# Layer-norm sums of 14 of 16 tiles made by ScalarE instead of VectorE, with a new order of operations, in an H3 and product-key-expert kernel

## The chip, the cores and the metric

One core of a Trainium2 chip runs the whole program. A core has five engines with a queue each, worked off in order: TensorE (PE in the profile; its weight loads are PEld), VectorE (DVE), ScalarE (ACT), GpSimd (POOL) and SyncE (SP). They run side by side and wait for one another by semaphores. Sixteen DMA engines move data between HBM and the core's memory SBUF; PE writes its products to PSUM. The metric is device microseconds (us) of one execution, lower is better.

## The reference: what is computed

The input `x` has 2048 tokens of 448 values. It is normalised over the 448 values, goes into two parts, and the output is the sum of `x` and both.

```python
xn = _layernorm(x)                         # (x - mean) / sqrt(var + 1e-5)
return x + _A_ref(xn, ...) + _B_ref(xn, ...)

# A: k gets a causal convolution of 4 taps, times v, then a causal convolution of
#    length 2048 in each channel by FFT, plus kv * ssm_D, times the gate xn
# B: 16 heads; s1, s2 = scores of xn's two query halves against 64 keys each
#    the best 2 of s1 and of s2 give 4 sums, the best 2 of these are the experts
g = _softmax(top_s)
act = _gelu(jnp.einsum("nd,nhkd->nhk", xf, u[top_e]))
out = jnp.einsum("nhk,nhk,nhkd->nd", g, act, v[top_e])
```

So every token reads 32 rows of `u` and 32 of `v` out of 4096.

## The kernel before

The tokens are 16 tiles (`T`) of 128. `acc` holds `x` and later the sum, `xn` the normalised input, both for all tiles. The program is straight code without loops on the chip; its order is made when it is built.

**Stages.** First the weights: the query projection is folded with the keys (L303 to L335) into `wh`, `wl` and `wr`, high and low halves of a 448 by 2048 matrix. Then the scores: for each tile `s_turn` transposes `xn` on PE (L347 into `px`), ACT splits it into `xh` and `xl` (L376 to L384), and `s_mm` makes four chunks of 512 scores (11 matmuls each, L363 to L367). `s_top` searches them on DVE: 8 times MAX8 (L407) and 8 times the index search (L405) a chunk. `s_pairs` picks the two experts of a head (L426 to L454), ACT makes the gates (`th`, `eg`, L434 to L437), PE places them (`pe`, L486), and ACT writes the rows' numbers `idx` and the gates `gt` (L469, L470). From then on POOL can gather a tile's rows.

Third come the experts, in 128 batches (8 a tile, named `b`). A batch is four gathers on POOL (L508) of 128 rows of `u` and `v` side by side, 0.46 MB each, into one of four buffers `uv`. DVE multiplies by the tokens' values (L540 for up to four gathers at once; L547 does one gather with its sum), ACT makes the sums (L559) and the gelu `ge` (L563), DVE the weight `w` (L574), ACT or DVE spreads it (`cc`, L589 or L579), PE adds up the rows of `v` (`pv`, L599 and L602), and with that the buffer is free. After a tile's last batch `vs`, `pf` and the sum into `acc` follow (L612, L621, L623).

Fourth, the convolution in two groups of 56 blocks of channels: SP loads `hkv` into `x1` (`c_load`, L639, seven loads of 0.8 MB, the first group's once the last tile's experts are placed), then taps, the transforms on PE and products of spectra on DVE (L738 to L744), the way back, and the gate into `acc`. The experts go on beside it.

**What sets the order.** Each stage is a stream of `Op`s with an engine, a cost in us, the keys that it waits for and a priority. `Planner.run` takes, engine by engine, the operation that can start first by these costs; among those that start within a little, the one with the smaller number in `PRIO`. The convolution's and the scores' numbers also change as the plan goes on: the scores are urgent while the gathers left to give out are fewer than `LEAD`, and `LATE` is added to the time at which a gather is taken to have landed before DVE's product is planned. The engines then do exactly that order; where data is late, all that stands behind it on the engine waits.

**What the change touches.** `norm(t0, t1)` normalises the tiles from `t0` to `t1`. It runs three times: tiles 0 and 1 ahead of all, tiles 2 to 5, and tiles 6 to 15. For each tile DVE makes mean and variance (L256 and L257); then, for the group at once, 3 + 16 + 1 small operations make `rstd` by Newton steps and `nmr` = -mean * rstd (L262 to L273, tiles `n`); then ACT writes `xn` tile by tile (L276).

```python
def stats(t=t):
    st = rp.tile([P, 6], F32, tag="st", name="st")
    nc.vector.bn_stats(st, acc[:, t, :])
    nc.vector.bn_aggr(mv[:, t, :], st)
yield Op("DVE", 0.78, stats, [("x", t0)])
```

Of the kernel before, what the change touches and what calls it, by code (L numbers as in the profile page):

```python
# [15 lines left out]
AF = mybir.ActivationFunctionType  # L16
ALU = mybir.AluOpType

P = 128
S, D, H, E = 2048, 448, 16, 64  # L20
# [6 lines left out]
VERBOSE = False  # L27
BEHIND = 0.2
PAD = 1.0
LEAD = 16  # L30
SPAN, AHEAD, WORK = 25.0, -0.010, 548.0


# [42 lines left out]

PRIO = {"c_back": 0.5, "c_delta": -0.1, "c_fin": 0.4, "c_fm": -0.4, "c_gate": -0.1, "c_hh": 0.5, "c_in": 0.5, "c_inv": 0.2, "c_mul": -0.2, "c_prod": -0.1, "c_spec": 0.3, "c_turn": 0.2, "c_zt": -0.5, "e_fold": -0.3, "e_gather": -0.5, "e_out": 0.5, "e_scale": -0.4, "e_spread": -0.5, "e_values": -0.5, "s_gate": 0.2, "s_put": -0.1, "s_top": 0.3, "s_turn": 0.1}


class Ring:
# [109 lines left out]
def parallel_kernel(ctx, tc, x, wq, kk, uv, hkv, const, fq, out):  # L192
    nc = tc.nc
# [14 lines left out]
    acc = ap.tile([P, NT, D], F32, name="acc")  # L208
    xn = ap.tile([P, NT, D], F32, name="xn")
# [5 lines left out]
    mv = ap.tile([P, NT, 2], F32, name="mv")  # L215
    rstd = ap.tile([P, NT], F32, name="rstd")
    nmr = ap.tile([P, NT], F32, name="nmr")
# [32 lines left out]
    def norm(t0, t1):  # L250
        sl, n = slice(t0, t1), t1 - t0
        va, y0, y1 = (ap.tile([P, n], F32, name=f"n{i}_{t0}") for i in range(3))
        for t in range(t0, t1):
            def stats(t=t):
                st = rp.tile([P, 6], F32, tag="st", name="st")
                nc.vector.bn_stats(st, acc[:, t, :])  # L256
                nc.vector.bn_aggr(mv[:, t, :], st)  # L257
            yield Op("DVE", 0.78, stats, [("x", t0)])


        def guess():
            nc.vector.tensor_scalar(va, mv[:, sl, 1], 1e-5, None, op0=ALU.add)  # L262
            nc.vector.tensor_scalar(y1.bitcast(I32), va.bitcast(I32), 1, None, op0=ALU.logical_shift_right)
            nc.vector.tensor_scalar(y0.bitcast(I32), y1.bitcast(I32), -1.0, float(0x5F3759DF), op0=ALU.mult, op1=ALU.add)
        yield Op("DVE", 0.5, guess)
        for i in range(4):
            def step(i=i):
                nc.vector.tensor_mul(y1, y0, y0)
                nc.vector.tensor_mul(y1, y1, va)
                nc.vector.tensor_scalar(y1, y1, -0.5, 1.5, op0=ALU.mult, op1=ALU.add)  # L270
                nc.vector.tensor_mul(y0 if i < 3 else rstd[:, sl], y1, y0)
            yield Op("DVE", 0.65, step)
        yield Op("DVE", 0.17, lambda: nc.vector.scalar_tensor_tensor(nmr[:, sl], mv[:, sl, 0], -1.0, rstd[:, sl], op0=ALU.mult, op1=ALU.mult),  # L273
                 key=("rstd", t0))
        for t in range(t0, t1):
            yield Op("ACT", 0.72, lambda t=t: nc.scalar.activation(xn[:, t, :], acc[:, t, :], AF.Identity, bias=nmr[:, t:t + 1], scale=rstd[:, t:t + 1]),  # L276
                     [("rstd", t0)], key=("xn", t))
# [253 lines left out]
    def e_dots():  # L531
        for b, (T, j, hf) in enumerate(order):
# [3 lines left out]
            if na:  # L536
                def go(b=b, T=T, j=j, na=na, begin=begin):
                    begin()
                    u = live["uv", b][:, :na, :D]
                    nc.vector.tensor_mul(u, live["xr", T, j][:, None, :D].broadcast_to([P, na, D]), u)  # L540
                yield Op("DVE", 0.1 + 0.46 * na, go, [(("land", b, na - 1), LATE), ("xr", T, j - j % 2)], key=("mul", b), rings=[(r_act, ("ge", b))])
            for c in range(na, 4):
                def go(b=b, T=T, j=j, c=c, na=na, begin=begin):
                    if c == 0:
# [3 lines left out]
                                                   accum_out=live["act", b][:, c:c + 1])  # L548
                yield Op("DVE", 0.63, go, [(("land", b, c), LATE), ("xr", T, j - j % 2)], key=("dot", b) if c == 3 else None,
                         rings=[(r_act, ("ge", b))] if c == 0 else [])  # L550
# [74 lines left out]
    def e_store(g):  # L625
        for T in range(NT):
            ch = slice(HALF * g, HALF * g + HALF)
            yield Op("SP", 0.06, lambda T=T: nc.sync.dma_start(out[T, :, ch], acc[:, T, ch]), [("sum", T), ("gt", g, GC // 8 - 1)], moved=1.15e5)
# [80 lines left out]
    def c_fm(g):  # L709
        for q in qs:  # L710
            def go(q=q):
                live["fm", g, q] = cp.tile([P, 2, P], F32, tag="fm", name="fm", bufs=FM)
                nc.sync.dma_start(live["fm", g, q].rearrange("p i n -> p (i n)"), fq[q])
            yield Op("SP", 0.06, go, [("cm", g, 4, 1)] if q == 0 else [], key=("fm", g, q), rings=[(r_fm, ("psu", g, q))], moved=1.35e5)

    def c_spec(g):

        for q in qs:
            def go(q=q):
                ps = live["psf", g, q] = ps_sc.tile([P, 512], F32, tag="sc", name="psf")  # L720
                nc.tensor.matmul(ps[:, :2 * HALF], live["fm", g, q][:, 0], x1[:, :, :, q, :].rearrange("p c t k -> p t c k"), start=True, stop=True)  # L721
            yield Op("PE", 0.85, go, [("fm", g, q)] + ([("x1", g, BC_LAST, t, 6) for t in range(2)] if q == 0 else []), key=("psf", g, q),
                     rings=[(r_sc, ("y", g, q))], lag=0.2)

    def c_hh(g):
        for q in qs:
            def go(q=q):
                hh = live["hh", g, q] = cp.tile([P, 2, HALF], F32, tag="hh", name="hh", bufs=HH)
                nc.scalar.activation(hh[:, 0], live["psf", g, q][:, :HALF], AF.Copy)
            yield Op("ACT", 0.28, go, [("psf", g, q)], key=("hh", g, q), rings=[(r_hh, ("psu", g, q))])  # L730
# [74 lines left out]

    LATE = 1.0
    r_ws, r_xh, r_eg, r_act, r_ge, r_w, r_cc, r_vs = Ring(2), Ring(2), Ring(2), Ring(3), Ring(3), Ring(3), Ring(2), Ring(1)
    live["by_act"], live["by_scale"] = 4, True  # L810
    nc.scalar.dma_start(kks, kk)
# [13 lines left out]
    plan.show("weights")  # L825
    experts = [plan.add(PRIO.get(s.__name__, 0.0), s()) for s in (e_gather, e_values, e_weigh, e_scale, e_spread, e_dots, e_gelu, e_out, e_fold)]
    stores = [plan.add(1, e_store(g)) for g in range(2)]
# [6 lines left out]
    def need(s):  # L834
        first = (0.2 if s in (s_mm, s_top) else 0.3 if s in (s_turn, s_split) else 0.4) - PRIO.get(s.__name__, 0.0)
        return lambda: (-1 if 32 * live["ready"] - plan.busy["POOL"] / 1.25 < LEAD else 2) - first
    plan.run([plan.add(need(s), s(pairs if s in (s_top, s_gate, s_place) else rest)) for s in scores])
# [11 lines left out]
    def turn():  # L849
        e = (plan.busy["POOL"] - begun) / (640.0 - begun)  # L850
        return -1 if plan.spent.get("conv", 0.0) / WORK < e + AHEAD else 1
    conv = []
    for g in range(2):
        for i, s in enumerate((c_load(g), c_delta(g), c_in(g, 0), c_store(g, 0), c_tap(g), c_prod(g), c_in(g, 1), c_store(g, 1),
                  c_fm(g), c_spec(g), c_hh(g), c_mul(g), c_inv(g), c_turn(g), c_back(g), c_zt(g), c_fin(g), c_gate(g))):
            conv.append(plan.add(lambda p=PRIO.get(s.__name__, 0.0): turn() + p, s, "conv"))
    plan.run(conv)
# [43 lines left out]
```

## Time and profile before

| | us |
|---|---|
| runs: median of 3 (lowest to highest) | 831.16 (830.13 to 832.6) |
| the profiled execution, its own time | 827.13 |
| its span, first to last instruction | 825.4 |
| scores of the first two tiles and norm of the rest | 57 to 82 |
| scores of tiles 2 to 15, experts beside them | 82 to 358 |
| convolution, group 0 then group 1, experts beside it | 358 to 825 |

The profile is of one execution. For each engine it gives busy time and instructions; a row of a group of instructions has line, engine, operation, output and inputs, count, then busy us and mean ns, then the idle time of the engine just before them and what ended it. A row of the timeline has start, duration, engine, line, operation, and in brackets the idle time before it with its releaser. Some views cut the span into stretches. In such rows `sc` are the scores, `mx` and `mi` maxima and indices, `n` the small tiles of the norm.

All 512 gathers together took this on POOL, with the idle time between them and what ended the most of it:

```profile
L508 POOL DMA_INDIRECT uv<-in_uv_dram,idx x512 | 491.5, 960 | 313.5 <-issue 95.6 <-ACT gt L470 67.0 <-PE pv L602 37.7
```

### The profile page before, as it was taken

What the parts mean: (1) busy time and instruction counts of PE and PEld (TensorE: products, weight loads), DVE (VectorE), ACT (ScalarE), POOL (GpSimd) and SP (SyncE); (2) the same over time, 40 slices, a digit from 0 to 9 for tenths busy, and PEclk for the clock granted to TensorE, in tenths of its full rate; (3) what the DMA queues carried; (4) which work ended last, traced back from release to release, by engine and by line L of the source; (5) the groups of instructions that cost most, each with busy time, mean ns of one, the idle gap of its engine ahead of it and who ended that gap; (6) DMA issues with size and microseconds to landing.
All of it is one profiled execution on the core that took longest, in us unless ns stands there. A gap on an engine that the chain in (4) does not pass through costs nothing.

```text
span 825.4 us, 16762 instructions
## 1 busy us (share of the span) xinstructions
PE 663.5 (80%) x5052; PEld 386.1 (47%) x5052; DVE 704.4 (85%) x2633; ACT 541.1 (66%) x1862; POOL 492.2 (60%) x518
## 2 busy tenths in 40 slices
PE   6994999899799999755876778886567878787884
PEld 2463565565456665413543343444244533333561
DVE  4379999999999999955898999984799779999774
ACT  4431897677777767665785676765378656766852
POOL 0004666576667666662777766666365776776670
PEclk9997799999999999976989999899698999999998
DMA  9955898899989998999999999999899999999995
GB/s 333 381 211 175 293 329 306 305 334 329 320 309 351 331 323 300 336 340 365 387 351 323 396 373 383 366 350 387 286 396 350 313 402 399 383 395 396 330 377 187
DMA packets 80554, 278.53 MB, mean 337 GB/s; under 512 B 10320, under 2 KB 47568, under 8 KB 80464
## 3 DMA queue, kind: packets, MB, share of 16 engines
q0 software_dynamic: 40960, 234.91, 77.2%
q1 hardware_dynamic: 39360, 42.41, 15.3%
q8 instruction: 41, 0.67, 0.3%
q14 instruction: 49, 0.40, 0.1%
q10 hardware_dynamic: 144, 0.13, 0.1%
HBM read 273.75 MB, written 3.67 MB: 336 GB/s over the span
## 4 chain that ended last, share of the span: by engine, by line
DVE 62%; PE 15%; DMA 14%; ACT 4%; issue 4%; DVEq 0%; SPq 0%; POOL 0%; POOLq 0%; ACTq 0%
DVE uv L540 21%; DVE mi L405 11%; DVE mx L407 7%; DMA uv<-in_uv_dram,idx 7%; DMA x<-in_hkv_dram 6%; PE pw L303 3%; ACT uv L559 3%; DVE hh L738 3%; DVE hh L739 3%; DVE hh L743 2%; PE pv L602 2%; PE ps L693 2%; DVE tap L660 2%; DVE tap L658 2%; DVE uv L547 2%
## 5 line engine op out<-in xcount | busy, mean ns | idle before, releaser
L508 POOL DMA_INDIRECT uv<-in_uv_dram,idx x512 | 491.5, 960 | 313.5 <-issue 95.6
L559 ACT ACTIVATE uv<-uv 128x448 f32<-128x448 f32 x455 | 256.5, 565 | 118.5 <-DVE uv L540 118.2
L540 DVE TENSOR_TENSOR uv<-xr,uv 128x1792 f32<-128x1792 f32 (+2 forms) x128 | 232.0, 1812 | 27.1 <-DMA uv<-in_uv_dram,idx 21.2
L602 PE MATMUL pv<-uv,cc 128*32 128x448 f32 x1024 | 140.6, 592 | 0.0
L405 DVE FIND_INDEX8 mi<-mx,sc 128x8 uint32<-128x64 f32 x512 | 105.4, 240 | 0.0
L753 PE MATMUL psu<-hh,fm 128*128 128x224 f32 x264 | 70.9, 396 | 21.2 <-DVE hh L744 18.1
L559 ACT ACTIVATION_READ_ACCUMULATOR uv<-uv 128x1 f32 x455 | 85.1, 187 | 0.0
L599 PE MATMUL pv<-uv,cc 128*1 128x4 bf16 x128 | 21.5, 168 | 79.0 <-DVE cc L579 63.0
L363 PE MATMUL sc<-wh,xh 128*128 128x512 f32 x192 | 82.1, 428 | 1.6 <-DVE mi L405 1.6
L753 PEld LDWEIGHTS psu<-hh,fm 128*128 128x128 f32 x264 | 48.8, 204 | 66.2 <-ACT uv L559 31.7
L407 DVE MAX8 mx<-sc 128x8 f32<-128x64 f32 x512 | 74.5, 230 | 3.1 <-PE sc L367 2.9
L365 PE MATMUL sc<-wh,xl 128*128 128x512 f32 x192 | 76.2, 397 | 0.0
L364 PE MATMUL sc<-wl,xh 128*128 128x512 f32 x192 | 76.2, 397 | 0.0
L693 PE MATMUL ps<-cst,x 128*64 128x132 f32 x896 | 64.4, 303 | 10.2 <-DVE x L675 6.3
L693 PEld LDWEIGHTS ps<-cst,x 128*64 128x64 f32 x896 | 56.4, 151 | 32.4 <-DVE x L675 8.2
L599 PEld LDWEIGHTS <-cc 128*1 128x1 bf16 x128 | 10.2, 80 | 129.0 <-DVE cc L579 92.0
L721 PE MATMUL psf<-x,fm 128*128 128x448 f32 x132 | 62.0, 563 | 0.4 <-DVE hh L744 0.2
L589 ACT ACTIVATE cc<-rep,w 128x32 f32<-128x32 f32 x196 | 46.4, 307 | 12.7 <-DVE w L574 12.6
L363 PEld LDWEIGHTS sc<-wh,xh 128*128 128x128 f32 x192 | 36.9, 192 | 34.1 <-issue 18.0
L405 DVE MATCH_VALUE_LOAD mi<-mx,sc 128x8 f32 x512 | 45.9, 90 | 0.0
L521 PE MATMUL xr<-xn,rep 32*128 32x448 f32 x128 | 34.5, 617 | 13.4 <-DVE uv L540 11.9
L761 ACT ACTIVATE x<-psu 128x224 f32<-128x224 f32 (+1 forms) x66 | 23.4, 354 | 27.9 <-PE psu L753 27.6
(98 smaller groups left out, 1028.3 us busy)
## 6 DMA issues: line engine op xcount, KB each, us to landing
wq<-in_wq_dram SPq DMA_DIRECT2D x16, 896.0 KB, 13.4
x<-in_hkv_dram SPq DMA_DIRECT2D x14, 780.0 KB, 14.8
fm<-in_fq_dram SPq DMA_DIRECT2D x66, 128.0 KB, 6.6
uv<-in_uv_dram,idx POOLq DMA_INDIRECT x512
out_dram<-acc SPq DMA_DIRECT2D x32, 112.0 KB, 1.8
acc<-in_x_dram SPq DMA_DIRECT2D x1, 2240.0 KB
acc<-in_x_dram SPq DMA_DIRECT2D x1, 896.0 KB
cst<-in_const_dram SPq DMA_DIRECT2D x1, 540.0 KB
```

Source lines behind the costliest of these rows:

```text
L363: nc.tensor.matmul(sc, xh[:, c, :], wh[:, c, ns], start=(c == 0), stop=False)
L364: nc.tensor.matmul(sc, xh[:, c, :], wl[:, c, ns], start=False, stop=False)
L365: nc.tensor.matmul(sc, xl[:, c, :], wh[:, c, ns], start=False, stop=False)
L405: nc.vector.max_index(mi[:, T % 2, 8 * n + j, :], m, sc[:, 64 * j:64 * j + 64])
L407: nc.vector.max(m, sc[:, 64 * j:64 * j + 64])
L508: made = nc.gpsimd.indirect_dma_start(live["uv", b][:, c, :], None, uv, bass.IndirectOffsetOnAxis(ap=idx[:, T, g:g + 1], axis=0)).ins
L540: nc.vector.tensor_mul(u, live["xr", T, j][:, None, :D].broadcast_to([P, na, D]), u)
L559: nc.scalar.activation(u, u, AF.Copy, accum_out=live["act", b][:, c:c + 1])
L602: nc.tensor.matmul(pv[32 * c:32 * c + 32, :D], cc[:, c, :], buf[:, c, D:], start=(hf == 0), stop=(hf == 1), tile_position=(0, 32 * c))
L693: nc.tensor.matmul(ps[64 * i:64 * i + 64, w * j:w * j + w], src, f1[:, i, :], start=True, stop=True, tile_position=(0, 64 * i))
L721: nc.tensor.matmul(ps[:, :2 * HALF], live["fm", g, q][:, 0], x1[:, :, :, q, :].rearrange("p c t k -> p t c k"), start=True, stop=True)
L753: nc.tensor.matmul(ps[:, :HALF], fm[:, 1], hh[:, i], start=(i == 0), stop=(i == 1))
```

## The change

For the two later groups of tiles `norm` no longer uses DVE's statistics. ACT reads a tile twice: a copy scaled by -1/448 whose accumulator gives minus the mean, and a square of the tile with that as its bias, whose accumulator gives the sum of squared differences. Both write their main output into `xn`, which the last step overwrites. The division by 448 goes into the first small operation on DVE, and the sign into the last; tiles 0 and 1 stay as they are. Two numbers of the planner and the table of priorities change too. The lines behind the new code are 12 further down.

```diff
-LEAD = 16
+LEAD = 12
...
-PRIO = {"c_back": 0.5, "c_delta": -0.1, "c_fin": 0.4, "c_fm": -0.4, "c_gate": -0.1, "c_hh": 0.5, "c_in": 0.5, "c_inv": 0.2, "c_mul": -0.2, "c_prod": -0.1, "c_spec": 0.3, "c_turn": 0.2, "c_zt": -0.5, "e_fold": -0.3, "e_gather": -0.5, "e_out": 0.5, "e_scale": -0.4, "e_spread": -0.5, "e_values": -0.5, "s_gate": 0.2, "s_put": -0.1, "s_top": 0.3, "s_turn": 0.1}
+PRIO = {"c_back": 0.5, "c_delta": -0.1, "c_fin": -0.1, "c_fm": -0.4, "c_gate": -0.1, "c_hh": 0.4, "c_in": 0.5, "c_inv": 0.2, "c_load": -0.4, "c_mul": -0.2, "c_prod": 0.1, "c_spec": 0.3, "c_store": 0.2, "c_tap": 0.5, "c_turn": 0.4, "c_zt": 0.3, "e_dots": 0.2, "e_fold": -0.3, "e_gather": -0.2, "e_gelu": -0.2, "e_out": -0.1, "e_scale": -0.3, "e_spots": -0.2, "e_spread": -0.5, "e_values": -0.5, "s_gate": 0.1, "s_put": -0.5, "s_split": 0.1, "s_top": 0.3, "s_turn": 0.1}
...
         for t in range(t0, t1):
+
+            def mean(t=t):
+                nc.scalar.activation(xn[:, t, :], acc[:, t, :], AF.Copy, scale=-1.0 / D, accum_out=mv[:, t, 0:1])
+            def squares(t=t):
+                nc.scalar.activation(xn[:, t, :], acc[:, t, :], AF.Square, bias=mv[:, t, 0:1], accum_out=mv[:, t, 1:2])
...
-            yield Op("DVE", 0.78, stats, [("x", t0)])
+            if t0 < 2:
+                yield Op("DVE", 0.78, stats, [("x", t0)])
+            else:
+                yield Op("ACT", 0.76, mean, [("x", t0)])
+                yield Op("ACT", 0.76, squares, key=("mv", t))
...
-            nc.vector.tensor_scalar(va, mv[:, sl, 1], 1e-5, None, op0=ALU.add)
+            if t0 < 2:
+                nc.vector.tensor_scalar(va, mv[:, sl, 1], 1e-5, None, op0=ALU.add)
+            else:
+                nc.vector.tensor_scalar(va, mv[:, sl, 1], 1.0 / D, 1e-5, op0=ALU.mult, op1=ALU.add)
...
-        yield Op("DVE", 0.5, guess)
+        yield Op("DVE", 0.5, guess, [("mv", t1 - 1)] if t0 >= 2 else [])
...
-        yield Op("DVE", 0.17, lambda: nc.vector.scalar_tensor_tensor(nmr[:, sl], mv[:, sl, 0], -1.0, rstd[:, sl], op0=ALU.mult, op1=ALU.mult),
+        yield Op("DVE", 0.17, lambda: nc.vector.scalar_tensor_tensor(nmr[:, sl], mv[:, sl, 0], -1.0 if t0 < 2 else 1.0, rstd[:, sl], op0=ALU.mult, op1=ALU.mult),
...
-    LATE = 1.0
+    LATE = 0.5
```

The order of the instructions is shown at three places. The first is ACT's queue from the split of tile 1 (`xh`, `xl_98`) to the first rows' numbers `idx`, before:

```order
L378 ACTIVATE xh<-px 64x128
L383 ACTIVATE xl_98<-px 128x384
L384 ACTIVATE xl_98<-px 64x128
L434 ACTIVATE th<-dd 128x16
L436 ACTIVATE eg<-th,half 128x16
L437 ACTIVATE eg<-th,half 128x16
L469 ACTIVATE idx<-pe 128x32
L470 ACTIVATE gt<-pe 128x32
```

and now:

```order
L390 ACTIVATE xh<-px 64x128
L256 ACTIVATE xn,mv<-acc 128x448
L258 ACTIVATE xn,mv<-acc,mv 128x448
...
L446 ACTIVATE th<-dd 128x16
L448 ACTIVATE eg<-th,half 128x16
L449 ACTIVATE eg<-th,half 128x16
...
L481 ACTIVATE idx<-pe 128x32
L482 ACTIVATE gt<-pe 128x32
```

Six tiles' means and squares (12 activations, with `xl_98` among them) now stand ahead of `th`, five activations between `eg` and `idx`, and the other 11 behind `gt`, around tile 1's `th` and `idx`.

The second is DVE's queue at the first products of the experts (`uv_751` is the second batch's, `uv_813` the third's; `w` are the weights), before:

```order
L574 TENSOR_TENSOR w_875<-ge_866,gt_90 128x4
L256 BN_STATS st_877<-acc_81 128x6
L257 BN_AGGR mv_86<-st_877 128x2
L256 BN_STATS st_894<-acc_81 128x6
L257 BN_AGGR mv_86<-st_894 128x2
L256 BN_STATS st_902<-acc_81 128x6
L257 BN_AGGR mv_86<-st_902 128x2
L256 BN_STATS st_906<-acc_81 128x6
L257 BN_AGGR mv_86<-st_906 128x2
L540 TENSOR_TENSOR uv_813<-xr_541,uv_813 128x4x448
L574 TENSOR_TENSOR w_937<-ge_919,gt_90 128x4
L262 TENSOR_SCALAR n0_6_538<-mv_86 128x10
```

and now, where `uv_759`, `uv_827` and `uv_866` are the second to fourth batch:

```order
L285 SCALAR_TENSOR_TENSOR nmr_88<-mv_86,rstd_87 128x10
L552 TENSOR_TENSOR uv_759<-xr_541,uv_759 128x4x448
L586 TENSOR_TENSOR w_883<-ge_869,gt_90 128x4
L552 TENSOR_TENSOR uv_827<-xr_541,uv_827 128x4x448
L586 TENSOR_TENSOR w_919<-ge_909,gt_90 128x4
L552 TENSOR_TENSOR uv_866<-xr_541,uv_866 128x4x448
L419 MAX mx_957<-sc_921 128x8 x4
L586 TENSOR_TENSOR w_966<-ge_952,gt_90 128x4
L419 MAX mx_957<-sc_921 128x8 x4
```

The statistics are gone between the products, and the small operations for tiles 6 to 15 are all done ahead of the second product instead of around the fourth. The weight of the third batch (`w_966`) now splits the first search of tile 2, so that search waits for ACT's gelu.

The third is DVE's queue in the scores of tile 3 (chunks `sc_1115`, `sc_1144`, `sc_1204`, `sc_1232`), before:

```order
L407 MAX mx_998<-sc_1115 128x8 x8
L540 TENSOR_TENSOR uv_1073<-xr_1010,uv_1073 128x4x448
L574 TENSOR_TENSOR w_1222<-ge_1202,gt_90 128x4
...
L540 TENSOR_TENSOR uv_1132<-xr_1010,uv_1132 128x4x448
...
L574 TENSOR_TENSOR w_1296<-ge_1276,gt_90 128x4
...
L540 TENSOR_TENSOR uv_1219<-xr_1315,uv_1219 128x4x448
L574 TENSOR_TENSOR w_1373<-ge_1338,gt_90 128x4
L405 MAX_INDEX mi_999<-mx_998,sc_1232 128x8 x8
```

and now (chunks `sc_1150`, `sc_1206`, `sc_1275`, `sc_1298`):

```order
L552 TENSOR_TENSOR uv_1032<-xr_970,uv_1032 128x4x448
L419 MAX mx_957<-sc_1150 128x8 x8
...
L552 TENSOR_TENSOR uv_1092<-xr_970,uv_1092 128x4x448
L586 TENSOR_TENSOR w_1234<-ge_1225,gt_90 128x4
...
L552 TENSOR_TENSOR uv_1164<-xr_1239,uv_1164 128x4x448
L586 TENSOR_TENSOR w_1289<-ge_1273,gt_90 128x4
...
L552 TENSOR_TENSOR uv_1221<-xr_1239,uv_1221 128x4x448
L586 TENSOR_TENSOR w_1337<-ge_1325,gt_90 128x4
...
L417 MAX_INDEX mi_958<-mx_957,sc_1298 128x8 x8
```

Four batches' products stand in tile 3's scores instead of three. The two orders are the same in this from here to the end of the scores: nine weights before tile 3's last search now, eight before; 48 before tile 15's last search now, 47 before. At the first product of the second group's spectra 99 batches are weighed instead of 100, at its first gate 120 in both.

## The prediction

> **What bounds the kernel now.** I read the page's busy shares and its chain first, then stretches of the span, and then single rows.
>
> ```profile
> PE 663.5 (80%) x5052; PEld 386.1 (47%) x5052; DVE 704.4 (85%) x2633; ACT 541.1 (66%) x1862; POOL 492.2 (60%) x518
> DVE 62%; PE 15%; DMA 14%; ACT 4%; issue 4%; DVEq 0%; SPq 0%; POOL 0%; POOLq 0%; ACTq 0%
> ```
>
> VectorE is busiest and carries most of the chain. The average hides stages, so the next view cuts the span: columns are the stretch, its length, busy time of PE, weight loads, DVE, ACT and POOL (each with its instructions), granted clock, share of the DMA engines, and rate.
>
> ```profile
> core 0: us, PE busy (x) PEld busy (x) DVE busy (x) ACT busy (x) POOL busy (x), PEclk, DMA share, GB/s
> 57.00:82.00 25.00, 14.29 (x121) 11.30 (x121) 23.83 (x178) 3.69 (x14) 9.61 (x11) 0.84 0.42 137
> 82.00:120.00 38.00, 35.73 (x163) 23.09 (x164) 36.79 (x171) 34.52 (x109) 23.61 (x25) 0.88 0.88 310
> 240.00:320.00 80.00, 77.80 (x471) 48.69 (x472) 79.19 (x474) 59.59 (x229) 54.39 (x58) 1.00 0.93 330
> 358.00:395.00 37.00, 20.49 (x171) 11.64 (x173) 19.10 (x39) 22.39 (x85) 17.30 (x18) 0.78 1.05 368
> 395.00:556.00 161.00, 127.29 (x895) 69.16 (x893) 148.81 (x298) 111.87 (x376) 115.35 (x120) 0.93 0.99 367
> 590.00:800.00 210.00, 167.93 (x1625) 96.18 (x1623) 186.02 (x377) 144.85 (x480) 148.71 (x155) 0.95 0.99 370
> ```
>
> Four regimes are seen. From 57 to 82 only DVE works hard, and ACT is nearly idle. From 82 to 120 DVE, PE **and ACT** are all above 90%. In the scores proper (240 to 320 stands for them) DVE has 0.8 us idle in 80 and PE 2.2. From 358 on the DMA engines are full (0.99 to 1.05), and 120 gathers took 161 us, 1.34 us each; a batch of four is 5.4 us there.
>
> ```profile
> DVE mx L407 <- PE sc L367: 1.0, 1, 1.0
> PE xr L521 <- DVE uv L540: 9.9, 7, 2.9
> ```
>
> These are the longest waits of DVE and of PE from 82 to 358: DVE's own row of work is the length of that stage, with PE close behind it.
>
> **What the change takes from DVE.**
>
> ```profile
> L256 DVE BATCH_NORM_STATS2 st<-acc 128x6 f32<-128x448 f32 x16 | 9.6, 602 | 2.9 <-DMA acc<-in_x_dram 2.9
> L257 DVE BATCH_NORM_AGGREGATE mv<-st 128x2 f32<-128x6 f32 x16 | 2.9, 182 | 0.5
> 57.50 0.61 DVE L256 BATCH_NORM_STATS2 st<-acc 128x6 f32<-128x448 f32 x1
> 60.55 0.17 DVE L262 TENSOR_SCALAR n<-mv 128x4 f32<-128x4 f32 x1
> 61.84 1.15 DVE L407 MAX8 mx<-sc 128x8 f32<-128x64 f32 x8
> 64.49 0.18 DVE L426 TENSOR_TENSOR best<-mx 128x32 f32<-128x32 f32 x1
> 78.34 0.15 DVE L268 TENSOR_TENSOR n<-n 128x4 f32<-128x4 f32 x1
> 80.86 0.61 DVE L256 BATCH_NORM_STATS2 st<-acc 128x6 f32<-128x448 f32 x1
> ```
>
> Four pairs take 57.50 to 60.55, that is 3.05 us, 0.76 each; 14 of the 16 pairs go, **10.7 us** of DVE's row. The first four do not give all of theirs.
>
> ```profile
> 59.47 0.39 PE L367 MATMUL sc<-wr,xl 128*128 128x512 f32 x1
> ```
>
> The scores of tile 0's last chunk end at 59.9, so DVE, free at 57.5, waits for them until 60.0: it comes to the MAX8 row of 61.84 only 1.84 earlier. Maxima and indices of a chunk are 2.65 (61.84 to 64.49). Tile 1 then ends at 76.5 instead of 78.34. Now all 20 small operations for tiles 2 to 5 follow (before, seven stood from 60.55 to 61.84 and 13 from 78.34 to 80.86: 3.8 us; I take 4.0): rstd is ready at 80.5 instead of 80.86. Behind that the other ten pairs are gone, too (7.6). So DVE's row is **8.2 us** shorter by the place where tile 2's scores are searched, if nothing else is late.
>
> **What ACT gets.** 28 activations with an accumulator, each second one behind the sum of the first. L559 is the nearest row, a copy of the same size with an accumulator.
>
> ```profile
> L559 ACT ACTIVATE uv<-uv 128x448 f32<-128x448 f32 x455 | 256.5, 565 | 118.5 <-DVE uv L540 118.2
> 97.25 0.56 ACT L559 ACTIVATE uv<-uv 128x448 f32<-128x448 f32 x1
> 97.94 0.20 ACT L563 ACTIVATE ge<-act 128x4 f32<-128x4 f32 x1
> 56.15 0.27 ACT L378 ACTIVATE xh<-px 64x128 fp32r<-64x128 f32 x1
> 65.21 0.21 ACT L434 ACTIVATE th<-dd 128x16 f32<-128x16 f32 x1 [7.42 <-DVE dd L429]
> 67.80 0.20 ACT L469 ACTIVATE idx<-pe 128x32 int32<-128x32 f32 x1 [1.83 <-PE pe L486]
> 77.41 0.22 ACT L434 ACTIVATE th<-dd 128x16 f32<-128x16 f32 x1 [9.33 <-DVE dd L429]
> 79.25 0.20 ACT L469 ACTIVATE idx<-pe 128x32 int32<-128x32 f32 x1 [1.08 <-PE pe L486]
> 80.97 2.71 ACT L276 ACTIVATE xn<-acc,nmr,rstd 128x448 f32<-128x448 f32 x4 [1.43 <-DVE nmr L273]
> ```
>
> One is 0.565; what reads an accumulator starts 0.69 after it (97.25 to 97.94). A mean and its squares are therefore 0.69 + 0.57 = 1.26, up to 1.37 if the bias costs what L276's operands do (2.71 / 4 = 0.68): 14 times, 17.6 to 19.2 us. ACT's idle time from 57.8 to 81 is 7.42 + 1.83 + 9.33 + 1.08 + 1.43 = 21.1, so they fit. I cost them at nothing, but for the queue: from 56.4, the end of xh, six tiles (7.6) and xl (0.5) stand ahead of tile 0's th, which starts at 64.5 although its input is ready at 63.4 (65.21 - 1.84). With th and the gates 0.7, and five more activations (3.1) ahead of idx, that comes at 68.3 to 69.2 instead of 67.80.
>
> ```profile
> 68.28 1.10 POOL L508 DMA_INDIRECT uv<-in_uv_dram,idx  x1 [66.97 <-ACT gt L470]
> 71.97 0.95 POOL L508 DMA_INDIRECT uv<-in_uv_dram,idx  x1 [0.30 <-issue]
> 82.41 2.02 DVE L540 TENSOR_TENSOR uv<-xr,uv 128x1792 f32<-128x1792 f32 x1
> 98.72 2.02 DVE L540 TENSOR_TENSOR uv<-xr,uv 128x1792 f32<-128x1792 f32 x1
> 115.37 1.15 DVE L407 MAX8 mx<-sc 128x8 f32<-128x64 f32 x8
> 131.93 0.24 DVE L426 TENSOR_TENSOR best<-mx 128x64 f32<-128x64 f32 x1
> 353.30 0.20 DVE L426 TENSOR_TENSOR best<-mx 128x64 f32<-128x64 f32 x1
> ```
>
> The first gather is so 0.5 to 1.4 us later than 68.28. Its data is not wanted before 80.5, so this costs nothing; without that cover it would cost the whole 1.4.
>
> **What is late next.** From 80.5 ACT has no gap. Up to the gelu of the fourth batch its new order holds 8 xn (5.4), 16 dot sums (9.0), 4 gelus (0.8), the cc of three batches, two xh, one xl and the table load.
>
> ```profile
> 84.09 0.49 ACT L376 ACTIVATE xh<-px 128x384 fp32r<-128x384 f32 x1 [0.40 <-PE px L347]
> 87.40 1.28 ACT L563 ACT_TABLE_LOAD   x1
> 90.84 0.94 ACT L589 ACTIVATE cc<-rep,w 128x32 f32<-128x32 f32 x4
> ```
>
> cc is 0.9 a batch (2.7), xh 0.95 with its three casts (84.09 to 85.04, where the next row starts; 1.9), xl half of that (0.5), the load 1.4 with its gap: 21.7 in all, so that gelu is there at 102.2. DVE's own work to the weight behind it is four products of 2.0, 20 small operations (4.1), one chunk (2.65) and 0.3: 95.6. **DVE waits 6.6 us for ACT**, most of the 8.2. From there two products (4.0) and three chunks (7.95) end tile 2 at 114.15, if PE has the third chunk by 108.9; before, the next tile's search began at 115.37: **1.2 us earlier**. In tile 3 the new order has four products where there were three. By these rows tile 3 was 16.56 = 4 x 2.65 + 3 x 2.0 before; now it is 18.7 and ends at 132.8 instead of 131.93, 0.9 later and one batch further. From there to the last index search both orders hold 39 weights and the same searches, and DVE, with 0.8 us idle in 80, can't go faster: the last search (ended at 353.30 before) comes about 0.9 us later, with 48 batches weighed instead of 47.
>
> **What the batch is worth behind 358.** In DVE's work 2.0 to 2.4 us; in gathers 4 x 1.25 (the pitch of POOL's issues, 0.95 + 0.30 in the row of 71.97) to 4 x 1.34, 5.0 to 5.4 us. Since the DMA share is 0.99 there, I take 5.0. The rest of the new order (PRIO, LEAD 12, LATE 0.5) does the same instructions: 89 products of four instead of 88, 200 cc on ACT instead of 196, two more dot sums. I take 0 and keep -6 to +6, about the sum of one regime's idle DVE time (161.00 - 148.81 = 12.2) half won or half added.
>
> Sum: +0.9 - 5.0 = **-4.1 us**. Against the profiled execution (827.13, 1.7 more than its span) that is 823.0. The median of the runs, 831.16, is 4.0 above that execution; the same difference gives **827.0**.
>
> **Two rules weighed.** The rate is 367 to 370 GB/s from 395 to 800. The Trainium skill, "DMA: Bandwidth & Descriptors", section "Where 436 GB/s comes from", puts the limit of HBM for one core at about 358 GB/s. By that rule this stage stands at its limit and gives nothing back, which is the rival "hidden" below, 831. The trace's rate is 9 to 12 GB/s above it, so here the limit is not that number.
>
> A mean with its squares is 1.26 us on ACT against 0.76 on DVE. The Trainium skill, "ScalarE: Activation LUTs", section "Rules for kernel authors", wants adds and multiplies on VectorE, not ScalarE. By that rule the 17.6 us would be added on ACT and 10.7 taken from DVE, 838 in all; ACT's 21.1 idle us at that place speak against it, and I give it no chance of its own.
>
> **The rivals.**
> - *All of it surfaces.* ACT's order lets DVE run on (shorter waits than I laid end to end), and the 8.2 stay: 7.0 more than forecast, 820. For it: DVE's chain share. Against: ACT at 34.52 of 38.
> - *Hidden.* PE, at 77.80 of 80, can't take the extra batch within the scores, whose end is then some 4 us later, and the full DMA engines set the rest: 831. For it: PE's row and the DMA share. Against: PE has 2.3 us of slack in 82 to 120.
> - *Slower: products placed too early.* LATE goes from 1.0 to 0.5, so the planner puts DVE's products half a us sooner behind their gathers.
>
> ```profile
> DVE uv L540 <- DMA uv<-in_uv_dram,idx: 20.9, 14, 4.1
> ```
>
> From 358 on DVE already waits 14 times for gathers, 1.5 us each, with 81 batches to do. Each further batch that stands 0.5 too early holds all that is behind it on DVE. It decides from eight such batches on (the 4.1); 20 cost 10 us and end 6 above: some 836, 835 with part of it hidden.
> - *The first products wait for the late idx:* 1.4 us, inside the forecast's range.
>
> **How the numbers follow.** Forecast 0.41 (its own range 823 to 830); all surfaces 0.15 (820); hidden 0.25 (831); slower 0.19 (835). A measurement of this kernel tells about 0.3% from no change, 2.5 us: faster is below 828.7, slower above 833.7. Of the forecast 0.35 is faster and 0.06 the same, so faster is 0.35 + 0.15 = 0.5, the same 0.06 + 0.25 = 0.31, slower 0.19. The range 817 to 835 takes in -6 on the forecast nearly whole and half of the slower case; about 0.15 is outside.
>
> **What would show it.** In the new profile: idx of tile 0 between 68 and 69.5 (right for the queue); DVE waiting for gelu and for PE's scores some 6 us in 82 to 120 (right for ACT as the wall; under 2 us, everything surfaces); the last index search near 354 with 48 weights ahead of it; the first wait for hkv's data one to two batches later; DVE's waits for gathers behind 358 near 21 us (over 30, the slower rival). I am wrong if the score stage ends more than 4 us earlier, or if the stage behind it changes its length by more than the batch.

## The result, and the profile after

| | kernel before | kernel after |
|---|---|---|
| median, 20 runs each | 830.23 us (825.6 to 838.15) | 825.0 us (821.66 to 830.99) |
| ratio | | 0.9945, 95% interval 0.9927 to 0.9964 |
| first profiled execution, own time | 827.13 | 829.65 |
| second profiled execution, own time | 829.95 | 821.42 |

The change makes the kernel 5.2 us faster; 827.0 was forecast. Single executions spread over some 10 us, and the first profile of the new kernel is of one of its longest, that of the old one of a short one. The stages are therefore read from two profiles of each.

First the busy times and the chain of waits of the new kernel's first profile, from its page:

```profile
PE 675.5 (82%) x5052; PEld 392.6 (47%) x5052; DVE 695.4 (84%) x2600; ACT 560.2 (68%) x1926; POOL 492.6 (60%) x518
DVE 49%; DMA 20%; PE 17%; ACT 5%; issue 4%; SPq 4%; POOL 1%; DVEq 0%; POOLq 0%; ACTq 0%
```

DVE is 9.0 us shorter (704.4 before), not the whole 10.7 of the working; what became of the other 1.7 stays open. ACT is 19.1 longer (541.1): the sums' two rows in this profile, L256 with 7.9 and L258 with 9.3, are 17.2 of that. The same stretches as before show where (PE, weight loads, DVE, ACT, POOL, granted clock, DMA share, GB/s):

```profile
57.00:82.00 25.00, 14.64 (x123) 11.39 (x121) 21.51 (x173) 21.04 (x70) 9.28 (x10) 0.86 0.39 131
82.00:120.00 38.00, 31.95 (x147) 19.06 (x148) 30.71 (x151) 37.12 (x118) 24.78 (x27) 0.82 0.90 316
240.00:320.00 80.00, 75.54 (x439) 46.30 (x438) 78.84 (x470) 60.02 (x229) 52.94 (x56) 0.94 0.91 323
395.00:556.00 161.00, 126.58 (x857) 67.50 (x854) 144.91 (x296) 108.51 (x367) 106.58 (x110) 0.90 0.96 347
590.00:800.00 210.00, 167.22 (x1599) 95.49 (x1597) 181.26 (x363) 143.50 (x475) 144.47 (x149) 0.94 0.99 369
```

From 57 to 82 ACT goes from 3.69 us of work to 21.04. From 82 to 120 DVE has 7.3 us without work (1.2 before) and ACT 0.9. From 395 to 556 this execution moved 347 GB/s against 367 before. The second execution moved 356 there (the second of the kernel before 360), and 373 from 590 on:

```profile
395.00:556.00 161.00, 127.38 (x868) 67.84 (x865) 148.45 (x304) 110.28 (x374) 112.30 (x115) 0.92 0.97 356
590.00:800.00 210.00, 168.39 (x1677) 97.38 (x1675) 181.08 (x360) 145.82 (x483) 146.83 (x151) 0.96 1.00 373
```

So these stretches alone don't tell where the 5 us come from. One count that differs is how much has been moved by the time at which the scores are done. For that one more stretch, from the start to 353.00, where the kernel before ends its last search; one row each of the kernel before (first profile, then second), and of the kernel after (first, second):

```profile
0.00:353.00 353.00, 312.25 (x1816) 188.60 (x1816) 317.50 (x1851) 233.28 (x832) 187.31 (x204) 0.96 0.88 310
```

```profile
0.00:353.00 353.00, 311.57 (x1816) 187.93 (x1818) 317.70 (x1854) 233.49 (x832) 188.01 (x204) 0.96 0.88 310
```

```profile
0.00:353.00 353.00, 315.79 (x1827) 190.96 (x1827) 307.38 (x1808) 253.81 (x900) 190.97 (x207) 0.96 0.88 313
```

```profile
0.00:353.00 353.00, 312.85 (x1827) 189.47 (x1827) 309.48 (x1813) 254.12 (x901) 192.27 (x209) 0.96 0.89 315
```

The kernel moves the same 278.5 MB in all. By 353 the new one has moved 3 to 5 GB/s more: 1.1 to 1.8 MB, which behind that point, at some 368 GB/s, would be worth **2.9 to 4.8 us** if the lead were kept to the end. In gathers (the x of POOL, six other instructions included) it is 3 to 5 more at this time. Whether the lead is kept is asked below, at the end of the first chip's runs.

### The profile page after: what moved, and what is told of

Read it like the earlier page. It is cut to its first block, busy times and chain, and to the rows that moved or that the text cites. A ratio compares the mean times of both kernels' runs of the same rounds, so it can differ in the third digit from the quotient of the medians.

```text
span 827.8 us, 16797 instructions
## 1 busy us (share of the span) xinstructions
PE 675.5 (82%) x5052; PEld 392.6 (47%) x5052; DVE 695.4 (84%) x2600; ACT 560.2 (68%) x1926; POOL 492.6 (60%) x518
## 4 chain that ended last, share of the span: by engine, by line
DVE 49%; DMA 20%; PE 17%; ACT 5%; issue 4%; SPq 4%; POOL 1%; DVEq 0%; POOLq 0%; ACTq 0%
DVE uv L552 18%; DMA uv<-in_uv_dram,idx 12%; DVE mi L417 9%; DMA x<-in_hkv_dram 7%; DVE mx L419 6%; SPq L651 4%; PE pw L315 4%; ACT uv L571 3%; PE pv L614 2%; PE psu L765 2%; DVE tap L672 2%; DVE tap L670 2%; DVE hh L751 2%; DVE hh L750 2%; DVE hh L755 2%
## 5 line engine op out<-in xcount | busy, mean ns | idle before, releaser
L552 DVE TENSOR_TENSOR uv<-xr,uv 128x1792 f32<-128x1792 f32 (+3 forms) x128 | 232.4, 1817 | 34.1 <-DMA uv<-in_uv_dram,idx 29.6
L614 PE MATMUL pv<-uv,cc 128*32 128x448 f32 x1024 | 144.9, 606 | 0.0
L705 PE MATMUL ps<-cst,x 128*64 128x132 f32 x896 | 69.2, 315 | 18.7 <-DVE x L687 6.5
L705 PEld LDWEIGHTS ps<-cst,x 128*64 128x64 f32 x896 | 60.4, 158 | 41.6 <-issue 20.4
L733 PE MATMUL psf<-x,fm 128*128 128x448 f32 x132 | 64.3, 575 | 2.5 <-DMA fm<-in_fq_dram 0.7
L611 PEld LDWEIGHTS <-cc 128*1 128x1 bf16 x128 | 10.2, 80 | 107.4 <-DVE cc L591 64.3
L533 PE MATMUL xr<-xn,rep 32*128 32x448 f32 x128 | 34.8, 620 | 13.8 <-DVE uv L552 10.7
L715 ACT ACTIVATE x<-ps 128x396 f32<-128x396 f32 (+1 forms) x84 | 35.4, 457 | 14.4 <-PE ps L705 14.4
L624 ACT ACTIVATE vs<-pv 128x448 f32<-128x448 f32 x64 | 34.1, 532 | 13.2 <-PE pv L614 12.9
```

The source lines that it names most:

```text
L614: nc.tensor.matmul(pv[32 * c:32 * c + 32, :D], cc[:, c, :], buf[:, c, D:], start=(hf == 0), stop=(hf == 1), tile_position=(0, 32 * c))
L705: nc.tensor.matmul(ps[64 * i:64 * i + 64, w * j:w * j + w], src, f1[:, i, :], start=True, stop=True, tile_position=(0, 64 * i))
```

## The experiments

Three theories stood against each other. **A**, that of the prediction: ScalarE becomes the wall, little of VectorE's 8.2 us is left, and the gain is that more batches are worked off beside the scores. **B**: the 8.2 us pass through, whatever the order. **C**: the sums are hidden, and the new order of the convolution makes the gain. In the expectations, the weights (batches) counted are those ahead of the first search of tile 15; the prediction's 47 and 48 were those ahead of its last one.

The experiments ran on two chips, and the chip matters: on the first the kernel before takes 831.08 us (18 runs; the 830.23 of the first comparison fits this chip), on the second 912.67 and in a later set 902.46 (35 runs each). The ratio is always to the kernel before on the same chip.

### First chip

**Both kernels again**, for a second profile.

> The kernel before once more. Where the program runs as in the first comparison: 830 us (825 to 838), VectorE almost without idle time from 240 to 320, and no idle time that nothing ends ('issue') on VectorE and ScalarE. If it takes some 912 us as in the last comparison, those pauses (31.6 us on VectorE there, 1.9 in the first profile) are there again.

> The new kernel once more: 825 us where the one before takes 830.
> Theory A (more batches in the scores): last index search 3 to 4 us later than before with 6 gathers more; the first group of the convolution as long as before, its start 3 to 4 later.
> Theory C (new order of the convolution): from the first group's first gate to the second group's first load 25 to 28 us against 37.6 before.

They took 829.95 and 821.42. The last search of the new kernel ended at 356.9 (first profile) and 354.5 (second), before at 353.3 and 353.0; 204 gathers had been given out by then instead of 198. The rows are the first small operation behind that search, of the new kernel's first and second profile:

```profile
356.85 0.21 DVE L438 TENSOR_TENSOR best<-mx 128x64 f32<-128x64 f32 x1
```

```profile
354.46 0.20 DVE L438 TENSOR_TENSOR best<-mx 128x64 f32<-128x64 f32 x1
```

That is A's picture of the scores: later by 1.2 to 3.9 us, but with 6 gathers more.

**The sums alone**: the new kernel, with the planner's numbers of before (PRIO's table too):

```diff
-LEAD = 12
+LEAD = 16
...
-    LATE = 0.5
+    LATE = 1.0
```

> The sums alone with the planner's numbers of before, once more. Expected as for the first run of it, where the kernel before takes 830: theory A about +4.4, 834.6 us (its order has two batches less beside the scores); theory B (VectorE's 8.2 us come off whatever the order) 825 or less; theory C 830 to 831.

Measured: 837.54 us, ratio 1.0077 (1.0049 to 1.0106), slower. VectorE is rid of the same 14 statistics as in the new kernel. B is refuted by this, and C's 830 to 831 too. But the planner laid the order anew here as well: this is not the sums in the order of before. What goes with the slower time is seen in the stretch to 353 and in the last gather:

```profile
0.00:353.00 353.00, 309.89 (x1837) 188.65 (x1837) 308.07 (x1834) 247.45 (x881) 183.47 (x199) 0.95 0.86 303
```

```profile
820.15 0.95 POOL L520 DMA_INDIRECT uv<-in_uv_dram,idx  x1 [0.30 <-issue]
```

The scores are done early, at 344.7, but with 188 gathers instead of 198. By 353 there are 7 GB/s less, 2.5 MB, 6.7 us behind. The planner used VectorE's free time for the scores and not for the experts, and less was moved beside them.

**The order alone**: LEAD, LATE and PRIO as in the new kernel, VectorE's statistics kept.

```diff
-LEAD = 16
+LEAD = 12
...
-    LATE = 1.0
+    LATE = 0.5
```

> The new numbers of the planner with VectorE's statistics, once more. Theory A: three batches more beside the scores, about 821 us; theory B: 830; theory C: 825 or less.

Measured: 829.0 us, ratio 0.9978 (0.9944 to 1.0011): no difference shown, and neither A's 821 nor C's 825 as a median. Its stretch to 353, its last gather and the last addition of the convolution's gate, and then these two rows of the new kernel's second profile:

```profile
0.00:353.00 353.00, 316.29 (x1842) 191.18 (x1842) 318.51 (x1845) 238.82 (x855) 193.95 (x210) 0.96 0.89 316
```

```profile
798.56 1.06 POOL L508 DMA_INDIRECT uv<-in_uv_dram,idx  x1 [0.30 <-issue]
...
810.04 0.69 DVE L803 TENSOR_TENSOR acc<-acc,fin 128x512 f32<-128x512 f32 x1
```

```profile
799.54 0.95 POOL L520 DMA_INDIRECT uv<-in_uv_dram,idx  x1 [0.30 <-issue]
...
808.04 0.69 DVE L815 TENSOR_TENSOR acc<-acc,fin 128x512 f32<-128x512 f32 x1
```

The order alone gets as much moved beside the scores as the new kernel does (316 GB/s, +6: 2.1 MB, 5.8 us). But it ends badly: the gate's last addition is 2 us later although the last gather is 1 us earlier, and the output stores that wait for it end the program 10.8 us behind it in both (821.5 and 819.5). From the last gather to the end it takes 22.9 us instead of 20.0. Sum: -5.8 + 2.9 = -2.9, measured -2.1.

The same sum for the three kernels, from these rows (the end behind the last gather is 825.4 - 805.4 = 20.0 before):

| kernel | moved by 353, worth | end behind the last gather | sum | medians apart |
|---|---|---|---|---|
| after (two profiles) | -2.9 and -4.8 | 0.0 | -2.9 and -4.8 | -5.2 |
| order alone | -5.8 | +2.9 | -2.9 | -2.1 |
| sums alone | +6.7 | -3.0 | +3.7 | +6.5 |

Set beside the medians, sign and order come out right and the sizes are within 3 us, less than single executions differ by. But the rows and the medians are not of the same executions. Against the span of the first profile of before (825.4) the profiled executions are 2.4 longer and 5.9 shorter (after), 3.9 shorter (order alone) and 11.7 longer (sums alone), so for each the sum misses by 1 to 8 us.

A needs one thing more: that the lead of 353 is still there later. The gathers that POOL has begun by four times, from all six profiles, say that it is not simply kept:

| us | before (two profiles) | after (two) | order alone | sums alone |
|---|---|---|---|---|
| 353 | 198, 198 | 201, 203 | 204 | 193 |
| 560 | 341, 339 | 337, 342 | 341 | 328 |
| 700 | 432, 431 | 429, 435 | 436 | 421 |
| 790 | 499, 497 | 497, 504 | 505 | 487 |

By 560, about where the second group of the convolution begins, the new kernel's lead is gone (4 behind in the first pair of profiles, 3 ahead in the second), and that of the order alone is 0 to 2. From 560 to 800 both kernels with the new numbers give out more, 169 and 171 (after) and 172 (order alone) against 167 in both profiles of before and 167 with the sums alone. That second lead is what C would look like, and so is this: from the first group's first gate addition to the end of the span it is 260 and 257 us in the new kernel and 253 with the order alone, against 267 and 268 before and 272 with the sums alone. So the count at 353 goes with the gain, but it is not shown to be its cause, and how much of the 5.2 us comes from the new order of the convolution stays open.

### Second chip

The same kernels gave no gain here.

> The new kernel once more, for a second profile beside the first, which was of one of its slower executions (829.65 against a median of 825.0). 825 us, 0.994 of the kernel before.
> Theory A: again the last index search 3 to 4 us later than before with 6 gathers more given out, and the first group of the convolution not longer than before (the 6 us lost there in the first profile are of that execution).
> Theory C: the stretch from the first group's first gate to the second group's first load is again about 12 us shorter than before (25.6 against 37.6), and that is what carries the gain.

> The sums of tiles 2 to 15 on ScalarE, but the planner with the numbers of before (LEAD 16, LATE 1.0, old PRIO). The planner lays everything anew: in DVE's order 41 batches' weights stand before tile 15's search where the kernel before has 43 (counted at the same row of both) and the new kernel 45.
> Theory A (a batch worked off beside the scores costs DVE 2.0 us there and saves 5.0 behind 358): score stage 1.6 shorter by the sums and 4.0 by two batches less, then 10 longer: about +4.4, 834.6 us.
> Theory B (DVE's 8.2 us come off the end whatever the order): 825 or less.
> Theory C (the new order does it, not the sums): 830 to 831, with the sums hidden.

> VectorE keeps all statistics; LEAD 12, LATE 0.5 and the new PRIO. The planner lays 46 batches' weights before tile 15's search (before 43, new kernel 45).
> Theory A: three batches more, +6 in the scores and -15 behind: -9, about 821 us, although nothing left VectorE.
> Theory B: 830, as before.
> Theory C: 825 or less.

Measured: the new kernel 914.62 us, ratio 1.0003 (0.9972 to 1.0034); the sums alone 1.0003 (0.9968 to 1.0038); the order alone 1.0045 (1.0017 to 1.0073). The new kernel's profile there shows that VectorE's row is not what the scores' length goes by:

```profile
240.00:320.00 80.00, 72.51 (x423) 44.82 (x422) 68.20 (x397) 52.30 (x197) 47.99 (x51) 0.98 0.88 290
```

VectorE is busy 68.20 us of 80 where it was busy 78.84 on the first chip, and the rate is 290 GB/s instead of 323. PE has 72.51, and no other engine has more. What stands still there is told at the end.

**Statistics back on VectorE, all else in the new order.** The planner still lays out ScalarE's operations, but what is emitted there is VectorE's pair, and the factor 1/448 and the sign go back:

```diff
-                yield Op("ACT", 0.76, mean, [("x", t0)])
-                yield Op("ACT", 0.76, squares, key=("mv", t))
+                yield Op("ACT", 0.76, lambda: None, [("x", t0)])
+                yield Op("ACT", 0.76, stats, key=("mv", t))
...
```

> The new kernel's planned order, every other instruction in its place, but the 14 statistics made by VectorE (bn_stats and bn_aggr, 0.76 us a pair) where ScalarE's squares stood; the factor 1/448 and the sign go back. So DVE has 10.7 us more, ACT 17.6 to 19 less, the order of all else is the same.
> Theory A: DVE's 7.3 us of idle time from 82 to 120 swallow most of it; the end is 0 to 3.4 later than the new kernel: 825 to 828.5.
> Theory B: 8 or more later: 833.
> Theory C: 825, and no difference beyond 0.3%.

> The new kernel's order with the statistics back on VectorE, where the kernel before takes 830. VectorE has 10.7 us more to do, of which 6.5 us of waiting for ScalarE and for the first gathers can take up a part (0.95, 0.99, 1.30, 0.79 and 2.28 us from 82 to 105).
> Theory A: tile 2 to 4's searches some 4 later than in the new kernel, the end 0 to 4 later: 825 to 829.
> Theory B: 8 later, 833.
> Theory C: no difference, 825.

It ran twice, both times on the second chip: 916.91 us, 1.0048 (1.0018 to 1.0078), and 907.84, 1.0052 (1.0020 to 1.0084).

**No sums at all, in the new order:** `mean` and `squares` emit nothing; mean 0 and variance 1 are set once instead. This kernel leaves the normalisation of tiles 2 to 15 out, so it gathers by other scores, as many rows as before.

> The new kernel's order with ScalarE's 28 activations left out (mean 0 and variance 1 are set instead, so tiles 2 to 15 aren't normalised). ScalarE has 17.6 to 19 us less from 57 to 80.
> Theory A: they lay in idle time, only tile 0's idx comes 1 earlier: 825 within 1.5 us, and VectorE still waits 4 us for the gelu from 82 to 105.
> Rival D (the sums' own load on ScalarE is what makes VectorE wait from 82 to 105): those waits are gone, search 4 earlier, 821.

901.65 us, 0.9994 (0.9965 to 1.0022). In this order statistics on VectorE cost about half a per cent against none, and sums on ScalarE (1.0003) can't be told from none. The two intervals alone would still allow some 4 us between them, which is what rival D (the sums' load on ScalarE makes VectorE wait) asks for. The traces speak against most of it: from 82 to 105 VectorE waits 2.5 us for ScalarE with the sums and 2.5 without them. Up to 120 it is 4.8 and 2.5, but all waits of VectorE together are 8.2 in both. So the 17.6 to 19.2 us lie in ScalarE's idle time, to within what these runs can tell. Between VectorE and ScalarE directly it is 2.3 us in the medians of one set (916.91 and 914.62), with intervals that overlap.

**The sums on ScalarE in the order of before**, with the 28 activations nearly where the new kernel has them, and **no statistics at all** in that order (mean 0 and variance 1 again; tiles 2 to 15 aren't normalised). The first one's edit:

```diff
...
             def stats(t=t):
+                if t >= 2:
+                    for s in {2: (2, 3), 3: (4, 5), 4: (6,), 5: (7,)}.get(t, ()):
+                        sums(s)
+                    return
...
+            def gates(T=group[0]):
+                live["gates", T]()
+                for t in (8, 9) if T == 0 else ():
+                    sums(t)
...
                 nc.scalar.activation(gt[:, T].rearrange("p (j k) -> p j k", k=8), pe[:, :, 1], AF.Copy)
+                for t in range(10, NT) if T == 0 else ():
+                    sums(t)
```

> The order of before, instruction by instruction; only the 14 statistics are taken out of VectorE's queue and the 28 activations put into ScalarE's, at the places where the new kernel has them (six tiles' ahead of tile 0's th, two ahead of idx, six behind gt).
> Theory A (ScalarE takes the place of VectorE as the wall from 80 to 105, so only 1 to 3 of the 8.2 us are left): last index search 1 to 3 earlier with the same 47 batches, 827 to 829 us.
> Theory B (VectorE's 8.2 us pass through): search at 345, 822 us.
> Theory C (hidden behind full DMA engines): search earlier, end the same, 830 to 831.

> The order of before with the 14 statistics left out altogether (mean 0 and variance 1 are set instead, so tiles 2 to 15 aren't normalised); ScalarE gets nothing. VectorE has 10.7 us less, ScalarE the same work.
> Theory A: ScalarE's row from 80 on is a wall of its own, so the same as with the sums on ScalarE: search 1 to 3 earlier, 827 to 829; that the sums themselves lie in ScalarE's idle time is right if the two kernels agree within 1.5 us.
> Theory B: 822.
> Theory C: 830 to 831.

With the sums on ScalarE 906.73 us, 1.0039 (1.0004 to 1.0075), slower; without any 901.8, 0.9991 (0.9961 to 1.0021), the same as before. One of its twelve runs took 1050.85; the median of the others is 900.9. Here is VectorE's queue in the first of them, and under it the stretch 57 to 82 of it and of the kernel without statistics:

```profile
57.17 0.22 DVE L416 FIND_INDEX8 mi<-mx,sc 128x8 uint32<-128x64 f32 x1
61.80 0.17 DVE L273 TENSOR_SCALAR n<-mv 128x4 f32<-128x4 f32 x1 [4.41 <-ACT xn L252]
```

```profile
57.00:82.00 25.00, 15.96 (x119) 12.13 (x119) 19.64 (x164) 20.03 (x64) 6.79 (x7) 0.83 0.27 81
```

```profile
57.00:82.00 25.00, 14.28 (x121) 11.34 (x121) 21.80 (x166) 3.74 (x15) 8.69 (x10) 0.83 0.43 140
```

In the order of before the small operations of tiles 2 to 5 stand in the middle of tile 0's search. There they now wait 4.41 us for ScalarE's sums, and tile 0's maxima behind them wait too. The first gather comes 4.1 us later (72.1 against 68.0), 81 GB/s move instead of 140, and the end is 4.9 us later (906.73 - 901.8; 5.8 against 900.9). Here the late start was not made up for: the kernel with the sums has begun 3 gathers fewer than the one without by 82 us (7 and 10), 3 fewer by 380 (196 and 199) and 2 fewer by 600. The new order puts those operations behind tile 1's search; in the old order the change was a loss on this chip.

Otherwise the count by a fixed time doesn't sort the kernels on this chip. By 380 the new kernel has begun 196 gathers and the sums alone 197 (ratio 1.0003 both), the order alone 197 (1.0045), the statistics in the new order 196 and 197 (1.0048, 1.0052).

No more than that was run: the fixed-order kernels on the first chip were not, so what the sums by themselves bring **there** stays open. There the medians of the new kernel and of the order alone are 4.0 apart, but the intervals of their ratios overlap (0.9927 to 0.9964, 0.9944 to 1.0011).

## Why the prediction came out as it did

On the first chip the time came as forecast, -4.1 foreseen and -5.2 measured. The steps up to tile 2 held. Behind them two terms were off in opposite directions, and the last step, that a batch worked off beside the scores is saved at the end, isn't shown: the lead was gone by 560. That the sum came out so near is in part luck.

**VectorE's row, 8.2 us shorter by tile 2: nearly right.** It is read at the product behind the small operations for tiles 6 to 15. Before, that is the row of 98.72 (98.27 in the second profile); now it starts at 87.69 and, in the second profile, here:

```profile
86.72 2.02 DVE L552 TENSOR_TENSOR uv<-xr,uv 128x1792 f32<-128x1792 f32 x1
```

Two products and two weights fewer stand ahead of it, some 4.0 us. What is left of the 11.03 and 11.55 is 7.0 and 7.5.

**ScalarE's sums 1.26 to 1.37 us a tile, in idle time: right.** In the new kernel's second profile, from one mean to the next:

```profile
56.10 0.58 ACT L256 ACTIVATE xn<-acc 128x448 f32<-128x448 f32 x1
56.58 0.19 ACT L256 ACTIVATION_READ_ACCUMULATOR xn<-acc 128x1 f32 x1
56.80 0.67 ACT L258 ACTIVATE xn<-acc,mv 128x448 f32<-128x448 f32 x1
57.38 0.19 ACT L258 ACTIVATION_READ_ACCUMULATOR xn<-acc,mv 128x1 f32 x1
57.47 0.56 ACT L256 ACTIVATE xn<-acc 128x448 f32<-128x448 f32 x1
```

One pair is 1.37; the squares start 0.70 behind the mean and they take 0.67 where the mean takes 0.56 to 0.58. The first idx came at 69.52 and 68.54, where 68.3 to 69.2 was forecast. The Trainium skill, "ScalarE: Activation LUTs", section "Rules for kernel authors", wants adds and multiplies on VectorE; by that rule the change would have been a loss. In the new order the runs show no cost of the sums beyond their 0.4%; in the order of before there is a loss, and with it VectorE's wait of 4.41 us for the sums.

**ScalarE as the wall from 80.5, 6.6 us of waiting: right in size, one fifth to one third of it for gathers.** VectorE's waits from 82 to 120 in the second profile:

```profile
DVE w L586 <- ACT ge L575: 4.1, 3, 2.3
DVE uv L552 <- DMA uv<-in_uv_dram,idx: 2.4, 3, 1.3
```

Together 6.5, of which 2.4 are for gathers (in the first profile 6.4, of which 1.3). The gelu of the fourth batch was forecast for 102.2:

```profile
101.98 0.21 ACT L575 ACTIVATE ge<-act 128x4 f32<-128x4 f32 x1
102.09 0.53 ACT L624 ACTIVATE vs<-pv 128x448 f32<-128x448 f32 x1
```

**Tile 3 ends 0.9 later: mis-sized.** "In tile 3 the new order has four products where there were three" was right, "now it is 18.7" was not: it took 20.6, from 114.65 to 135.28, and tile 2 had gained 0.3 instead of 1.2 (114.94 in the second profile of before). In the timeline of that tile:

```profile
126.64 1.15 DVE L419 MAX8 mx<-sc 128x8 f32<-128x64 f32 x8 [0.62 <-PE sc L379]
129.02 2.02 DVE L552 TENSOR_TENSOR uv<-xr,uv 128x1792 f32<-128x1792 f32 x1 [1.23 <-DMA uv<-in_uv_dram,idx]
```

VectorE had run ahead of the gathers and of PE, and two waits, 1.9 us together, came into a tile in which I had counted none. So the tile ended 3.8 to 4.1 later. The last search came 1.2 to 3.9 later where 0.9 was forecast; "with 0.8 us idle in 80, can't go faster" held in one execution and not in the other, where the lag shrank to 1.5.

**One batch, 5.0 us: mis-sized the other way.** The order has one weight more ahead of the last search, 48 instead of 47, as forecast. But POOL had given out 6 gathers more, one and a half batches: it was two gathers further ahead of the weights than before (12 instead of 10). And a gather behind 353 costs more than the pitch of 1.25 that I took: in the first profile of before, the 314 behind the last search are given out from 353.3 to 806.3, 1.44 us each. At that price six are 8.7 us, against 1.2 to 3.9 of a later search. Weights in VectorE's order are so a poor count of what has been moved: theory A's three further batches of the order alone (821 expected) were 6 gathers by 353, not 12. And the lead isn't carried to the end: by 560 it was 3 at most. The prediction's own sign for this was that the stage behind the scores changes by no more than the batch. From the last search to the end of the span it took 472.1 us before and 471.0 now in the first profiles, 475.2 and 465.0 in the second. The second pair changes by 10.2, twice the batch, so by that sign this step was wrong there.

**The rest of the order, 0 with -6 to +6: the term that stays open.** With the planner's old numbers the same sums made the kernel 6.5 us slower. From 560 to 800 the kernels with the new numbers give out 2 to 5 gathers more than before, 2.9 to 7.2 us at 1.44 each; this belongs to the term taken as 0. That the change doesn't work without its tables I had not put down as a step.

**The signs and rivals.** The first wait for hkv's data came two batches later (52 weights ahead of it instead of 50), as foreseen. *All surfaces* didn't happen. *Slower by LATE 0.5* didn't either; its mark was over 30 us of waits for gathers behind 358, and these are the rows of the two profiles (20 of its batches would have ended at 837 by the prediction's numbers, not at 836):

```profile
DVE uv L552 <- DMA uv<-in_uv_dram,idx: 25.9, 17, 6.3
```

```profile
DVE uv L552 <- DMA uv<-in_uv_dram,idx: 20.9, 14, 5.4
```

The time of *hidden*, no change, came on the second chip; that it came by PE isn't shown there. The Trainium skill's limit of about 358 GB/s ("DMA: Bandwidth & Descriptors", section "Where 436 GB/s comes from"), by which it was weighed, is no limit here: the second profile moved 373 GB/s from 590 to 800.

## What to carry to other kernels

Where the DMA engines are full behind a stage and not within it, an engine's shorter row need not be worth its length: count what a change gets moved, and count it at several times, since a lead seen at one can be gone at the next. Work moved to an idle engine brings its consumers a new wait: look where they stand in the other queue, and move them behind what must not be late, as the small operations were moved here behind tile 1's search. Where a planner lays the program anew, run the edit and the planner's numbers apart before the gain is put down to either.

## What was not expected of the hardware

The second chip runs the same program 9 to 10% longer (912.67 and 902.46 against 831.08), and not because the instructions compared are slower: a gather is 945 ns on POOL on both, a product of 1792 is 2.01 us on both. There the engines also stand still for nothing that the profile shows. From 82 to 356, the waits of VectorE in the new kernel, first on the second chip, then on the first (whole view):

```profile
...
DVE mi L417 <- issue: 3.7, 7, 1.2
...
DVE mx L419 <- issue: 2.9, 6, 0.9
DVE mx L419 <- remote: 2.8, 1, 2.8
...
```

```profile
DVE w L586 <- ACT ge L575: 4.8, 3, 2.3
DVE uv L552 <- DMA uv<-in_uv_dram,idx: 3.7, 5, 1.3
DVE mx L419 <- PE sc L379: 0.9, 2, 0.6
DVE uv L552 <- issue: 0.3, 1, 0.3
```

In all it is 32.3 us against 9.7. Rows with "issue" are 8.3 of that and rows with "remote", for which the profile names no engine of this core, 5.8; the others are waits for other engines, which may themselves have paused. The pauses shown lie in the middle of searches, between two instructions of VectorE that need nothing from elsewhere. Added up over the span, the rows with "issue" are 31.6 us on VectorE and 33.4 on ScalarE there, 0.5 and 0 on the first chip; in the chain of waits "issue" has 10% instead of 4%. The granted clock doesn't explain it (0.917 there, 0.919 here), nor do the queues that load instructions: 41 and 49 packets there, 41 and 50 here, 0.3 and 0.1% of the DMA engines' time on both. What does stays open. So a gain of half a per cent, measured on one chip, was not there on another.
